# Gate and up matmuls as pairs of 64 rows, with an exchanged copy of the normalised input

## The chip, the cores and the metric

The kernel runs on one core of one Trainium2 chip. The metric is device time in microseconds (us) of one execution, and lower is better. Times given for a kernel are medians over several executions; a profile is one further execution, with its own time.

## The reference, cut to what matters

Two branches work on the same normalised input, and their sum is added to the input. D is 576, S is 2048, F is 4608; all inputs and the output are bf16.

```
x  = A_x                                  # [1, 2048, 576]
xn = layernorm(x)                         # over the last axis
q, k, v = split(xn @ A_wqkv)              # 32 heads of 18
# each position attends to itself and 7 earlier ones, 2 apart
logits[s, w] = q[s] . k[s - 2w] * 18**-0.5      # -1e9 where s - 2w < 0
o = sum_w softmax(logits)[s, w] * v[s - 2w]
g = silu(xn @ B_w_gate)                   # 576 -> 4608
u = xn @ B_w_up                           # 576 -> 4608
out = x + o @ A_wo + (g * u) @ B_w_down   # 4608 -> 576
```

## The kernel before, in words

Tokens are held as 16 rows (`r`) of 128 partitions: token 16p + r is partition p of row r. Four rows make a block `tt` of 512 tokens (`TT`), and there are four blocks.

**First stage.** Each row is normalised, transposed on TensorE (L213) and copied by ScalarE into `xnT`: 128 partitions by 5 groups of features by 2048 tokens. The first four groups hold features 0 to 511. The last 64 features stand twice in the fifth group, on partitions 0 to 63 and on 64 to 127. Then come the K and Q projections (`p_full`, L225, and `p_rem`, L232), row by row, and after them V in four groups of four rows. K and V go to staging buffers that lie in the memory of `hT`; `halo` (L281 to L286) copies them from there, shifted by one partition, into the rings `Kr` and `Vr`, and to a scratch in DRAM (`kv_d`) from which later blocks are read back (`ring_load`, L291). There are three staging buffers in turn, so ScalarE's copy of a V group out of PSUM (L247) waits until the copies out of the buffer that it writes have landed.

**Gate and up.** For each block `tt`, a loop runs over nine chunks `ch` of 512 columns of the 4608. Each chunk has four parts `j` of 128 columns. A part needs gate and up, each [128 columns] x [512 tokens], summed over 576 features: four matmuls of 128 features (`g_full`, L415) and one of 64 (`g_rem`, L425) for each of the two. In `g_rem` gate reads partitions 0 to 63 and up partitions 64 to 127, so that two matmuls stand in the two halves of TensorE's array at the same time. The eight short matmuls of a chunk stand together: parts 0 and 1 do their long matmuls first, then come all the short ones, then the long ones of parts 2 and 3. Gate and up of a part go to the two banks of one PSUM tile (a ring of four tiles of two banks). `g_evac` then applies silu to gate on ScalarE (L431), copies up on ScalarE (L432), and multiplies both on VectorE into `hT` (L433).

**Weights.** `load_gu` brings a chunk's weights into one of two slots of `gu`: 512 rows of gate and of up as [128 partitions, 4, 512] each (L163, L164), and the last 64 rows of gate on partitions 0 to 63 and of up on 64 to 127 (L165, L166). All four are on the queue of SP (SyncE), in program order. The load for chunk it + 2 is issued after the matmuls of chunk `it`, and waits for them. In block 0 two loads of `w_down` (L169) follow behind each.

**VectorE's own work.** The sliding attention is a list of pieces (`Filler`), which `dve.pump` puts between other VectorE work, with costs written out by hand. The list of block tt + 1 is added in chunk 1 of block tt.

**Down and output.** After the nine chunks of a block, the attention's output is transposed (L474, copied by L478), and for each of four rows 36 matmuls of `w_down` (L489) and five of `A_wo` (L492) go into one PSUM tile for each half of the 576 columns. VectorE adds the residual `xr` into a tile `ot` (L498), and SP stores it (L499). `xr` is one buffer, loaded in chunk 4 of each block.

Of the kernel before, what the change touches and what calls it, by code (L numbers as in the profile page):

```python
# [9 lines left out]
bf16 = mybir.dt.bfloat16  # L10
f32 = mybir.dt.float32
ACT = mybir.ActivationFunctionType
ALU = mybir.AluOpType
# [4 lines left out]
P = 128  # L18
H, DH, W, DIL = 32, 18, 8, 2
D = H * DH  # L20
HALF = D // 2
# [8 lines left out]
NTT = R // RT  # L30
TT = RT * P
NRING = HALO + RT
FC = 4
NSLOT = 2
# [31 lines left out]
def kernel(  # L66
# [11 lines left out]
    nc = tc.nc  # L78
# [4 lines left out]
    NCH = NF // FC  # L83

    x_v = A_x.rearrange("b (p r) d -> p (b r) d", r=R)
    out_v = out.rearrange("b (p r) d -> p (b r) d", r=R)

    const = ctx.enter_context(tc.tile_pool(name="const", bufs=1))
    big = ctx.enter_context(tc.tile_pool(name="big", bufs=1))
    tmp = ctx.enter_context(tc.tile_pool(name="tmp", bufs=1))  # L90
# [9 lines left out]
    xnT = big.tile([P, KT, S], bf16, name="xnT")  # L100
# [9 lines left out]
    ssum = big.tile([P, RT, H], f32, name="ssum")  # L110
    gu = big.tile([P, NSLOT, 9, FC * P], bf16, name="gu")
    xr = big.tile([P, RT, D], bf16, name="xr")
    kv_d = dram.tile([2, NTT - 1, P, RT * D], bf16, name="kv_d")


# [17 lines left out]


    nc.gpsimd.memset(eps_t[:], EPS)
    wz = tmp.tile([P, D], bf16, name="ot", tag="ot", bufs=3)
    nc.vector.memset(wz[:], 0.0)

    def load_w3(eng, m):
        src = A_wqkv[:, m * D:(m + 1) * D]  # L140
        eng.dma_start(wq3[m], src[0:512, :].rearrange("(kt kp) n -> kp kt n", kp=P))
        eng.dma_start(wq3r[m][0:64, :], src[512:576, 0:HALF])
        eng.dma_start(wq3r[m][64:128, :], src[512:576, HALF:D])
# [16 lines left out]
    def load_gu(it):  # L160
        ch, slot = it % NCH, it % NSLOT
        fc = slice(ch * FC * P, (ch + 1) * FC * P)
        nc.sync.dma_start(gu[:, slot, 0:4, :], B_w_gate[0:512, fc].rearrange("(kt kp) n -> kp kt n", kp=P))  # L163
        nc.sync.dma_start(gu[:, slot, 4:8, :], B_w_up[0:512, fc].rearrange("(kt kp) n -> kp kt n", kp=P))  # L164
        nc.sync.dma_start(gu[0:64, slot, 8, :], B_w_gate[512:576, fc])  # L165
        nc.sync.dma_start(gu[64:128, slot, 8, :], B_w_up[512:576, fc])  # L166

    def load_wd(ch):
        nc.sync.dma_start(wd[:, ch * FC:(ch + 1) * FC, :],  # L169
                          B_w_down[ch * FC * P:(ch + 1) * FC * P, :].rearrange("(f p) j -> p f j", p=P))  # L170

    def new_ps(name):
        return ps.tile([P, 2, 512], f32, name=name, tag="ps")
# [81 lines left out]
    def p_units(units, hooks):  # L255


        n = len(units) // 2
        ts = []
        for i in range(n):  # L260
            ts.append(new_ps("qkv_ps"))
            p_full(*units[i], ts[i], True)
            hooks[i]()
        for i in range(n, len(units)):
            ts.append(new_ps("qkv_ps"))
        for i, (m, r) in enumerate(units):
            p_rem(m, r, ts[i], i >= n)
        for i in range(n):
            p_evac(*units[i], ts[i])
        for i in range(n, len(units)):  # L270
            p_full(*units[i], ts[i], False)
            p_evac(*units[i], ts[i])
            hooks[i]()
# [20 lines left out]
    dve = Filler()  # L294
# [92 lines left out]
    for r in range(R):  # L387
        p_units([(1, r), (0, r)], [ahead, ahead if r == 2 else none])
        if r == 0:
            nc.sync.dma_start(xc_b[2], x_v[:, 8:12, :])  # L390
            nc.sync.dma_start(xc_b[3], x_v[:, 12:16, :])
            load_w3(nc.sync, 2)
    nc.vector.memset(Kr[0:1, 0:HALO, :], 0.0)
    nc.vector.memset(Vr[0:1, 0:HALO, :], 0.0)
    load_gu(0)
    load_gu(1)
    chain(0)
    for i in range(4):
# [6 lines left out]
    wd_order = [8, 0, 1, 2, 3, 4, 5, 6, 7]  # L405
    ring_ps = {}

    def g_full(tt, ch, j, first):
        slot = (tt * NCH + ch) % NSLOT
        t = ring_ps[j]  # L410
        tok = slice(tt * TT, (tt + 1) * TT)
        fc = slice(j * P, (j + 1) * P)
        for b in range(2):
            for kt in range(4):
                nc.tensor.matmul(t[:, b, :], gu[:, slot, 4 * b + kt, fc], xnT[:, kt, tok],  # L415
                                 start=(first and kt == 0), stop=(not first and kt == 3))

    def g_rem(tt, ch, j, first):
        slot = (tt * NCH + ch) % NSLOT
        t = ring_ps[j]  # L420
        tok = slice(tt * TT, (tt + 1) * TT)
        fc = slice(j * P, (j + 1) * P)
        for b in range(2):
            rows = slice(64 * b, 64 * b + 64)
            nc.tensor.matmul(t[:, b, :], gu[rows, slot, 8, fc], xnT[rows, 4, tok], start=first, stop=not first)  # L425

    def g_evac(ch, j):
        t = ring_ps[j]
        sg = tmp.tile([P, TT], bf16, name="sg", tag="sg", bufs=4)
        uc = tmp.tile([P, TT], bf16, name="uc", tag="uc", bufs=4)  # L430
        nc.scalar.activation(sg[:], t[:, 0, :], ACT.Silu)  # L431
        nc.scalar.copy(uc[:], t[:, 1, :])  # L432
        nc.vector.tensor_tensor(hT[:, ch * FC + j, :], sg[:], uc[:], op=ALU.mult)  # L433

    for tt in range(NTT):
        for ch in range(NCH):
            it = tt * NCH + ch
            for j in (0, 1):
                ring_ps[j] = new_ps("g_ps")
                g_full(tt, ch, j, True)  # L440
            for j in (2, 3):
                ring_ps[j] = new_ps("g_ps")
            g_rem(tt, ch, 0, False)
            g_rem(tt, ch, 1, False)
            g_rem(tt, ch, 2, True)
            g_rem(tt, ch, 3, True)
            g_evac(ch, 0)
            dve.pump(1.4)
            g_evac(ch, 1)
            dve.pump(1.4)  # L450
            g_full(tt, ch, 2, False)
            g_evac(ch, 2)
            dve.pump(1.4)
            g_full(tt, ch, 3, False)
            g_evac(ch, 3)
            dve.pump(1.4)
            if it + NSLOT < NTT * NCH:
                load_gu(it + NSLOT)
            if tt == 0:
                for _ in range(2):  # L460
                    if wd_order:
                        load_wd(wd_order.pop(0))
            if ch == 4:
                nc.sync.dma_start(xr[:], x_v[:, RT * tt:RT * tt + RT, :])
            if ch == 1 and tt < NTT - 1:
                chain(tt + 1)
        dve.drain(lambda: chains[0] > tt)

        def o_transp(pair):
            pt = ps.tile([P, 2, 8 * P], bf16, name="ot_ps", tag="ps")  # L470
            for q in range(2):
                r = RT * tt + 2 * pair + q
                for k, (c0, n) in enumerate(OCH):
                    nc.tensor.transpose(pt[0:n, q, k * P:(k + 1) * P], QO[:, r, c0:c0 + n], ident[:])  # L474
            for q in range(2):
                r = RT * tt + 2 * pair + q
                for a, b, n in ((0, 3, 128), (3, 5, 96)):
                    nc.scalar.copy(oT[0:n, a:b, r * P:(r + 1) * P],  # L478
                                   pt[0:n, q, a * P:b * P].rearrange("p (k t) -> p k t", t=P))

        o_transp(0)
        o_transp(1)
        for sub in range(RT):
            r = RT * tt + sub
            t = new_ps("d_ps")
            for h in range(2):
                cols = slice(h * HALF, (h + 1) * HALF)
                for f in range(NF):
                    nc.tensor.matmul(t[:, h, 0:HALF], hT[:, f, sub * P:(sub + 1) * P], wd[:, f, cols],  # L489
                                     start=(f == 0), stop=False)  # L490
                for k, (c0, n) in enumerate(OCH):
                    nc.tensor.matmul(t[:, h, 0:HALF], oT[0:n, k, r * P:(r + 1) * P], wo[0:n, k, cols],  # L492
                                     start=False, stop=(k == KT - 1))
            dve.pump(8.5)
            ot = tmp.tile([P, D], bf16, name="ot", tag="ot", bufs=3)
            for h in range(2):
                cols = slice(h * HALF, (h + 1) * HALF)
                nc.vector.tensor_tensor(ot[:, cols], t[:, h, 0:HALF], xr[:, sub, cols], op=ALU.add)  # L498
            nc.sync.dma_start(out_v[:, r, :], ot[:])  # L499


# [28 lines left out]
```

## Time and profile before

| | |
|---|---|
| median of 3 executions | 534.65 us (532.63 to 535.03) |
| the profiled execution | 535.35 us, its span 533.2 us |
| TensorE busy | 520.2 us, 98% of the span |
| granted TensorE clock, mean | 0.996 |
| VectorE busy | 333.4 us, 63% |
| ScalarE busy | 222.1 us, 42% |
| DMA | 70.39 MB, mean 132 GB/s |
| gate and up, long matmuls (L415) | x1120, 379 ns each |
| gate and up, short matmuls (L425) | x288, 379 ns each |

The span is the time from the first to the last instruction of the profiled execution; what lies around it is 535.35 - 533.2 = 2.15 us. Matmuls are pipelined: the duration of one (379 ns) is longer than the distance to the next, so that rates are read from distances between starts. A few matmul records are missing (1120 of 1152 long ones are there). "Idle before" is an engine's idle time ahead of an instruction, with what ended it. SPq is SP's sequencer, on which DMAs are issued.

### The profile page before, as it was taken

To read this page: it belongs to the slowest core of one execution; us is meant where nothing else is said; L and a number is where in the kernel's file an instruction comes from. 1 tells how busy PE (TensorE), PEld (TensorE's weight loads), DVE (VectorE), ACT (ScalarE), POOL (GpSimd) and SP (SyncE) were. 2 spreads that over 40 slices of the span, in tenths; PEclk is the share of its full clock that TensorE was granted. 3 is DMA by queue.
4 is the path that set the end of the run, shared out by engine and by line. 5 is a ranking of instruction groups with operands and counts; after the bars stand their busy time and mean duration, and the time that the engine had idled before them with its cause. 6 is when DMAs were issued, how large, how long until landed. Compare 5 with 4: busy or idle time off the path is not lost.

```text
span 533.2 us, 8296 instructions
## 1 busy us (share of the span) xinstructions
PE 520.2 (98%) x3375; PEld 300.8 (56%) x3407; DVE 333.4 (63%) x474; ACT 222.1 (42%) x431; POOL 9.7 (2%) x25
## 2 busy tenths in 40 slices
PE   6999989999999999999999999999999999999997
PEld 2677754444477754444577644444777544445775
DVE  4765977698899868898798127986991121221010
ACT  2677545656440035455600074466400354555000
POOL 6000000000000000000000000000000000000000
PEclk9899999999999999999999999999999999999999
DMA  8332798996620115554601035545200145540000
GB/s 280 119 134 90 217 301 263 339 306 201 216 90 23 57 49 185 177 176 136 222 13 57 23 97 171 171 149 169 90 12 23 58 131 177 184 129 0 12 12 22
DMA packets 58229, 70.39 MB, mean 132 GB/s; under 512 B 3768, under 2 KB 54072, under 8 KB 58192
## 3 DMA queue, kind: packets, MB, share of 16 engines
q1 hardware_dynamic: 56928, 68.55, 40.4%
q0 software_dynamic: 576, 0.66, 0.4%
q10 hardware_dynamic: 688, 0.66, 0.4%
q8 instruction: 26, 0.43, 0.4%
q14 instruction: 11, 0.09, 0.1%
HBM read 58.69 MB, written 5.90 MB: 121 GB/s over the span
## 4 chain that ended last, share of the span: by engine, by line
PE 92%; DMA 5%; SPq 1%; issue 1%; DVE 0%; ACT 0%; DVEq 0%; ACTq 0%
PE g_ps L415 47%; PE d_ps L489 26%; PE g_ps L425 7%; PE qkv_ps L225 6%; PE d_ps L492 4%; DMA gu<-in_B_w_up_dram 2%; DMA Vr<-hT 1%; PE qkv_ps L232 1%; DMA wd<-in_A_x_dram 1%; PE pt L213 1%; PE ot_ps L474 1%; DMA hT<-in_A_wqkv_dram 1%; SPq L282 0%; SPq L286 0%; DVE wd L200 0%
## 5 line engine op out<-in xcount | busy, mean ns | idle before, releaser
L415 PE MATMUL g_ps<-xnT,gu 128*128 128x512 bf16 x1120 | 252.5, 379 | 4.4 <-ACT hT L247 1.8
L415 PEld LDWEIGHTS <-gu 128*128 128x128 bf16 x1152 | 109.8, 98 | 144.0 <-issue 17.3
L431 ACT ACTIVATE sg<-g_ps 128x512 bf16<-128x512 f32 x144 | 87.1, 605 | 157.6 <-PE g_ps L425 123.2
L489 PE MATMUL d_ps<-wd,hT 128*128 128x288 bf16 x1152 | 146.4, 286 | 0.0
L489 PEld LDWEIGHTS <-hT 128*128 128x128 bf16 x1152 | 112.4, 98 | 28.5
L433 DVE TENSOR_TENSOR hT<-sg,uc 128x512 bf16<-128x512 bf16 x144 | 60.4, 420 | 106.8 <-ACT uc L432 106.0
L316 DVE TENSOR_REDUCE PP<-PP 128x64 f32<-128x1152 bf16 x64 | 85.1, 1347 | 0.4
L432 ACT CAST uc<-g_ps 128x512 bf16<-128x512 f32 x144 | 85.1, 591 | 0.0
L498 DVE TENSOR_TENSOR ot<-d_ps,xr 128x288 bf16<-128x288 f32 x32 | 13.1, 451 | 64.6 <-PE d_ps L492 64.6
L225 PE MATMUL qkv_ps<-hT,xnT 128*128 128x288 bf16 x384 | 52.0, 291 | 0.1
L225 PEld LDWEIGHTS <-xnT 128*128 128x128 bf16 x384 | 36.2, 99 | 14.5 <-issue 5.0
L343 DVE TENSOR_TENSOR PP<-Vr,A 128x2304 bf16<-128x2304 bf16 (+1 forms) x35 | 43.4, 1252 | 0.5
L311 DVE TENSOR_TENSOR PP<-QO,Kr 128x2304 bf16<-128x2304 bf16 (+1 forms) x35 | 43.4, 1248 | 0.3
L425 PE MATMUL g_ps<-xnT,gu 64*128 64x512 bf16 x288 | 37.4, 379 | 0.0
L348 DVE TENSOR_TENSOR PP<-PP 128x2304 bf16<-128x2304 bf16 x24 | 32.5, 1355 | 0.4
L431 ACT ACT_TABLE_LOAD x5 | 6.4, 1283 | 54.3 <-PE g_ps L425 54.2
L492 PE MATMUL d_ps<-wo,xnT 128*128 128x288 bf16 (+1 forms) x160 | 24.9, 286 | 0.0
L425 PEld LDWEIGHTS <-gu 64*128 64x128 bf16 x288 | 11.1, 94 | 23.8 <-issue 15.3
L492 PEld LDWEIGHTS <-xnT 128*128 128x128 bf16 (+1 forms) x160 | 15.7, 98 | 3.9
L188 DVE BATCH_NORM_STATS2 stats<-wd 128x6 f32<-128x288 bf16 x32 | 13.0, 449 | 3.8 <-DMA wd<-in_A_x_dram 3.8
L247 ACT CAST hT<-qkv_ps 128x288 bf16<-128x288 f32 x32 | 10.6, 416 | 10.8 <-DMA Vr<-hT 4.9
L336 ACT ACTIVATE PP<-PP 128x1024 f32<-128x1024 f32 x4 | 4.2, 1057 | 24.8 <-DVE PP L332 24.8
(40 smaller groups left out, 167.4 us busy)
## 6 DMA issues: line engine op xcount, KB each, us to landing
gu<-in_B_w_gate_dram SPq DMA_DIRECT2D x36, 512.0 KB, 3.6
gu<-in_B_w_up_dram SPq DMA_DIRECT2D x36, 512.0 KB, 5.1
wd<-in_B_w_down_dram SPq DMA_DIRECT2D x9, 576.0 KB, 5.7
kv_d<-hT SPq DMA_DIRECT2D x6, 576.0 KB, 4.9
gu<-in_B_w_gate_dram SPq DMA_DIRECT2D x36, 64.0 KB, 4.9
gu<-in_B_w_up_dram SPq DMA_DIRECT2D x36, 64.0 KB, 4.5
xr<-in_A_x_dram SPq DMA_DIRECT2D x4, 576.0 KB, 5.4
out_dram<-ot SPq DMA_DIRECT2D x16, 144.0 KB, 1.8
```

Of the source, the lines that this page charges most:

```text
L225: nc.tensor.matmul(t[:, h, 0:HALF], xnT[:, kt, r * P:(r + 1) * P], wq3[m][:, kt, h * HALF:(h + 1) * HALF], start=(first and kt == 0), stop ...
L311: nc.vector.tensor_tensor(prod[:, a:b], QO[:, RT * tt + a:RT * tt + b, :], Kr[:, s:s + b - a, :], op=ALU.mult)
L316: nc.vector.tensor_reduce(L[:, w, rs], prod[:, rs].rearrange("p r (h d) -> p r h d", d=DH), axis=AX.X, op=ALU.add)
L343: nc.vector.tensor_tensor(dst[:, a:b], Vr[:, s:s + b - a, :].rearrange("p r (d h) -> p r d h", h=H), A[:, w, a:b].unsqueeze(2).to_broadcas ...
L348: nc.vector.tensor_tensor(dst, acc, pv, op=ALU.add)
L415: nc.tensor.matmul(t[:, b, :], gu[:, slot, 4 * b + kt, fc], xnT[:, kt, tok], start=(first and kt == 0), stop=(not first and kt == 3))
L425: nc.tensor.matmul(t[:, b, :], gu[rows, slot, 8, fc], xnT[rows, 4, tok], start=first, stop=not first)
L431: nc.scalar.activation(sg[:], t[:, 0, :], ACT.Silu)
L432: nc.scalar.copy(uc[:], t[:, 1, :])
L433: nc.vector.tensor_tensor(hT[:, ch * FC + j, :], sg[:], uc[:], op=ALU.mult)
L489: nc.tensor.matmul(t[:, h, 0:HALF], hT[:, f, sub * P:(sub + 1) * P], wd[:, f, cols], start=(f == 0), stop=False)
L492: nc.tensor.matmul(t[:, h, 0:HALF], oT[0:n, k, r * P:(r + 1) * P], wo[0:n, k, cols], start=False, stop=(k == KT - 1))
```

## The change

All the gate and up matmuls are now short ones of 64 features. The 576 rows of a weight are nine pieces of 64; gate's nine pieces lie on partitions 0 to 63 of a slot and up's nine on partitions 64 to 127. A part `j` is nine pairs: one matmul of gate in the upper half of the array and one of up in the lower half.

A gate piece with an odd number needs features that `xnT` holds on partitions 64 to 127, and an up piece with an even number needs some that it holds on 0 to 63. For these there is `xsw`, a copy of the first four groups of a block of `xnT` with its two halves exchanged, made by two DMAs from SBUF to SBUF: once in the first stage (at r = 5) and then after the gate and up part of each block but the last. The order of the pairs takes those that need no `xsw` first.

`load_gu` becomes two DMAs, one of 64 partitions for gate and one of 64 partitions for up, 576 KB each. The parts of a chunk run one after the other, with `g_evac` and `dve.pump(1.4)` behind each. The buffers `sg` and `uc` go from four to three. The residual is added in place in `xr`, which is then stored, and `ot` is gone; the zeros for the first matmuls lie in `xr` as well.

```diff
+    xsw = big.tile([P, 4, TT], bf16, name="xsw")
...
-    wz = tmp.tile([P, D], bf16, name="ot", tag="ot", bufs=3)
-    nc.vector.memset(wz[:], 0.0)
+    wz = xr[:, 0, :]
+    nc.vector.memset(wz, 0.0)
...
     def load_gu(it):
         ch, slot = it % NCH, it % NSLOT
         fc = slice(ch * FC * P, (ch + 1) * FC * P)
-        nc.sync.dma_start(gu[:, slot, 0:4, :], B_w_gate[0:512, fc].rearrange("(kt kp) n -> kp kt n", kp=P))
-        nc.sync.dma_start(gu[:, slot, 4:8, :], B_w_up[0:512, fc].rearrange("(kt kp) n -> kp kt n", kp=P))
-        nc.sync.dma_start(gu[0:64, slot, 8, :], B_w_gate[512:576, fc])
-        nc.sync.dma_start(gu[64:128, slot, 8, :], B_w_up[512:576, fc])
+        nc.sync.dma_start(gu[0:64, slot], B_w_gate[:, fc].rearrange("(c p) n -> p c n", p=64))
+        nc.sync.dma_start(gu[64:128, slot], B_w_up[:, fc].rearrange("(c p) n -> p c n", p=64))
+
+    def load_xsw(tt):
+        tok = slice(tt * TT, (tt + 1) * TT)
+        nc.sync.dma_start(xsw[0:64], xnT[64:128, 0:4, tok])
+        nc.sync.dma_start(xsw[64:128], xnT[0:64, 0:4, tok])
...
+        if r == 5:
+            load_xsw(0)
...
-    def g_full(tt, ch, j, first):
+    def g_mm(tt, ch, j):
         slot = (tt * NCH + ch) % NSLOT
         t = ring_ps[j]
         tok = slice(tt * TT, (tt + 1) * TT)
         fc = slice(j * P, (j + 1) * P)
-        for b in range(2):
-            for kt in range(4):
-                nc.tensor.matmul(t[:, b, :], gu[:, slot, 4 * b + kt, fc], xnT[:, kt, tok],
-                                 start=(first and kt == 0), stop=(not first and kt == 3))
-
-    def g_rem(tt, ch, j, first):
...
-        for b in range(2):
-            rows = slice(64 * b, 64 * b + 64)
-            nc.tensor.matmul(t[:, b, :], gu[rows, slot, 8, fc], xnT[rows, 4, tok], start=first, stop=not first)
+        lo, hi = slice(0, 64), slice(64, P)
+        order = [(0, 1), (2, 3), (4, 5), (6, 7), (8, 8), (1, 0), (3, 2), (5, 4), (7, 6)]
+        for i, (cg, cu) in enumerate(order):
+            xg = xsw[lo, cg // 2, :] if cg % 2 else xnT[lo, cg // 2, tok]
+            xu = xnT[hi, cu // 2, tok] if cu % 2 or cu == 8 else xsw[hi, cu // 2, :]
+            for b, rows, c, x in ((0, lo, cg, xg), (1, hi, cu, xu)):
+                nc.tensor.matmul(t[:, b, :], gu[rows, slot, c, fc], x, start=(i == 0), stop=(i == 8))
...
-        sg = tmp.tile([P, TT], bf16, name="sg", tag="sg", bufs=4)
-        uc = tmp.tile([P, TT], bf16, name="uc", tag="uc", bufs=4)
+        sg = tmp.tile([P, TT], bf16, name="sg", tag="sg", bufs=3)
+        uc = tmp.tile([P, TT], bf16, name="uc", tag="uc", bufs=3)
...
-            for j in (0, 1):
+            for j in range(FC):
                 ring_ps[j] = new_ps("g_ps")
-                g_full(tt, ch, j, True)
-            for j in (2, 3):
-                ring_ps[j] = new_ps("g_ps")
-            g_rem(tt, ch, 0, False)
-            g_rem(tt, ch, 1, False)
-            g_rem(tt, ch, 2, True)
-            g_rem(tt, ch, 3, True)
-            g_evac(ch, 0)
-            dve.pump(1.4)
-            g_evac(ch, 1)
-            dve.pump(1.4)
-            g_full(tt, ch, 2, False)
-            g_evac(ch, 2)
-            dve.pump(1.4)
-            g_full(tt, ch, 3, False)
-            g_evac(ch, 3)
-            dve.pump(1.4)
+                g_mm(tt, ch, j)
+                g_evac(ch, j)
+                dve.pump(1.4)
...
         dve.drain(lambda: chains[0] > tt)
+        if tt + 1 < NTT:
+            load_xsw(tt + 1)
...
-            ot = tmp.tile([P, D], bf16, name="ot", tag="ot", bufs=3)
             for h in range(2):
                 cols = slice(h * HALF, (h + 1) * HALF)
-                nc.vector.tensor_tensor(ot[:, cols], t[:, h, 0:HALF], xr[:, sub, cols], op=ALU.add)
-            nc.sync.dma_start(out_v[:, r, :], ot[:])
+                nc.vector.tensor_tensor(xr[:, sub, cols], t[:, h, 0:HALF], xr[:, sub, cols], op=ALU.add)
+            nc.sync.dma_start(out_v[:, r, :], xr[:, sub, :])
```

More of the change, by code (lines that the diff above doesn't have):

```diff
@@ L412, in g_full @@
         fc = slice(j * P, (j + 1) * P)
-        for b in range(2):
-            for kt in range(4):
-                nc.tensor.matmul(t[:, b, :], gu[:, slot, 4 * b + kt, fc], xnT[:, kt, tok],
-                                 start=(first and kt == 0), stop=(not first and kt == 3))
-    def g_rem(tt, ch, j, first):
[L419 to L422, printed above, removed]
-        for b in range(2):
-            rows = slice(64 * b, 64 * b + 64)
-            nc.tensor.matmul(t[:, b, :], gu[rows, slot, 8, fc], xnT[rows, 4, tok], start=first, stop=not first)
+        lo, hi = slice(0, 64), slice(64, P)
[5 more added lines that the diff above has]
+                nc.tensor.matmul(t[:, b, :], gu[rows, slot, c, fc], x, start=(i == 0), stop=(i == 8))
     def g_evac(ch, j):
         t = ring_ps[j]
-        sg = tmp.tile([P, TT], bf16, name="sg", tag="sg", bufs=4)
-        uc = tmp.tile([P, TT], bf16, name="uc", tag="uc", bufs=4)
+        sg = tmp.tile([P, TT], bf16, name="sg", tag="sg", bufs=3)
+        uc = tmp.tile([P, TT], bf16, name="uc", tag="uc", bufs=3)
         nc.scalar.activation(sg[:], t[:, 0, :], ACT.Silu)
```

## The prediction, made before the result was known

> **What bounds the kernel now.** I read the page's busy times and its chain of waits first.
>
> ```profile
> span 533.2 us, 8296 instructions
> PE 520.2 (98%) x3375; PEld 300.8 (56%) x3407; DVE 333.4 (63%) x474; ACT 222.1 (42%) x431; POOL 9.7 (2%) x25
> ...
> PE 92%; DMA 5%; SPq 1%; issue 1%; DVE 0%; ACT 0%; DVEq 0%; ACTq 0%
> ```
>
> TensorE (PE) carries 92% of the chain that ends last, so the question is the distance between its matmuls, and whether anything else will be late. For the distances I took the timeline of one chunk in block 1:
>
> ```profile
> 201.20 1.04 PE L425 MATMUL g_ps<-xnT,gu 64*128 64x512 bf16 x8
> ...
> 202.17 7.08 PE L415 MATMUL g_ps<-xnT,gu 128*128 128x512 bf16 x32
> ...
> 204.97 0.37 SPq L163 DMA_DIRECT2D gu<-in_B_w_gate_dram  x1
> ...
> 205.83 0.37 SPq L164 DMA_DIRECT2D gu<-in_B_w_up_dram  x1
> ...
> 206.81 0.59 SPq L166 DMA_DIRECT2D gu<-in_B_w_up_dram  x1
> ...
> 209.19 1.04 PE L425 MATMUL g_ps<-xnT,gu 64*128 64x512 bf16 x8
> ```
>
> Columns are start, length, engine, line. A chunk lasts 209.19 - 201.20 = 7.99 us. Long matmuls follow each other at (7.08 - 0.38) / 31 = 0.216 us (0.38 is the length of one, 379 ns). Eight short ones are four pairs: (1.04 - 0.38) / 3 = 0.22 us from pair to pair. A pair costs what one long matmul costs, so nine pairs are no more work than eight long ones and a pair. What is lost now are the changes between the two kinds: short to long 0.97 - 4 x 0.216 = 0.106 us, long to short 7.02 - 32 x 0.216 = 0.108 us, together 0.21 us per chunk.
>
> **What goes on TensorE.** 36 chunks x 0.21 = 7.6 us are removed; two changes per block stay, into pairs and back to whole-array transposes: 4 x 0.21 = 0.8 us. A chunk becomes 36 x 0.216 = 7.78 us. Sum: -6.8 us, all on the path.
>
> Can the sequencer keep up? A pair is four instructions (two weight loads), 54 ns each. In the K and Q stage one row takes 2.70 us (runs of L225 start at 28.69, 31.38, 34.08 in the chain) for 25 matmuls and 25 weight loads, 54 ns each, with no gap on PE. It holds there, and I book nothing; the trace shows no row beyond that rate in a long run.
>
> **What comes instead: the refill of a slot.** Now gate's large load leaves at 204.97, when the last gate matmul is through, 0.86 us before up's. Interleaved pairs free both at the end, so both leave at about 205.83, 0.2 us after the chunk's end (202.17 + 16 x 0.216 = 205.63). They must land before the next chunk is over, 7.78 us after that end. Today the last small load leaves at 206.81 and lands 4.5 us later (page's median for L166): 211.3, 5.7 us after the end, with 2.3 us to spare. But the new loads fill 64 partitions each, and the trace has no long transfer of that shape. The nearest rows, in windows of the DMA columns (share, GB/s, at the end of each line):
>
> ```profile
> 312.00:313.00 1.00, 1.00 (x7) 0.41 (x6) 0.42 (x1) 0.18 (x1) 0.00 (x0) 1.00 1.03 363
> 313.00:314.00 1.00, 0.95 (x5) 0.47 (x5) 0.00 (x0) 0.00 (x0) 0.00 (x0) 1.00 1.07 366
> ...
> 36.25:37.50 1.25, 1.25 (x15) 0.76 (x12) 1.13 (x4) 1.04 (x2) 0.00 (x0) 1.00 1.07 269
> 38.50:39.50 1.00, 1.00 (x13) 0.61 (x12) 0.59 (x3) 0.57 (x3) 0.00 (x0) 1.00 1.05 429
> 72.00:74.00 2.00, 2.00 (x21) 1.44 (x21) 1.93 (x3) 0.00 (x0) 0.00 (x0) 1.00 1.02 229
> ```
>
> All are saturated (share about 1). The first two are today's weight loads over 128 partitions. The third is the K halo copy over 112 partitions, shifted by one; the fourth the store of the same buffer over 128. Same packets of 4608 B, but their mean length is 291 ns against 180: where the partitions do not spread evenly, packets wait for each other and the rate falls to 269/429 = 0.63. The fifth, V halos, falls to 229/429 = 0.53. Bounds for the new loads: 366 GB/s (no loss; today's 64-row remainders, 64 packets each at the end of a refill, have a median packet of about 51 ns there against 46 before, nearly that) down to 0.53 x 366 = 195. I take 0.63, 230 GB/s: a long load that uses one half of the partitions is nearer to the uneven copy than to a few packets among others.
>
> [...]
>
> A chunk's weights are 1.18 MB: 3.2 us at 366, 5.1 at 230, 6.0 at 195. Start and landing around the data are today 211.3 - 205.83 - 3.2 = 2.3 us. So the refill lands 0.2 + 2.3 + 5.1 = 7.6 us after the chunk's end, against 7.78: just in time. L164's landings scatter (median 5.1 us, some over 6), so I book 0.13 us of waiting per refill: 21 refills in blocks 1 to 3, 2.7 us; at 366 nothing, at 195 0.2 + 2.3 + 6.0 - 7.78 = 0.7 us, 0.8 with the scatter.
>
> **Block 0** also loads `w_down`, 1.18 MB per chunk over 128 partitions, behind each refill on the same queue: 5.1 + 3.2 = 8.3 us of transfers per 7.78 us of chunk. For four chunks 0.55 us each, 1.6 us for the read-back of K (0.59 MB) among them, 0.4 us for the rest: +4.2 us.
>
> **The start of gate and up.** The first two chunks' weights (2.36 MB) are queued at 58 us, ahead of V's halo copies, and the DMA share is about 1 from 57 to 83 us. ScalarE waits for one of those copies, and TensorE for ScalarE:
>
> ```profile
> 75.75 2.52 ACT L247 CAST hT<-qkv_ps 128x288 bf16<-128x288 f32 x8 [4.91 <-DMA Vr<-hT]
> ...
> 76.50 3.61 PE L415 MATMUL g_ps<-xnT,gu 128*128 128x512 bf16 x15 [1.83 <-ACT hT L247]
> ```
>
> At 230 GB/s the weights take 10.3 us instead of 6.4, and the copies behind them land 3.8 us later. Two issues per chunk instead of four let SP reach the copies earlier; that can give between nothing and the stall's 1.83 us, and I take 0.8. Sum +3.0 us; without the rate loss -0.8. One more cost can hide here: after PE's idle time at 10 to 12 us the granted clock was 0.50 at 14 to 16 us. If a stall of 5 us did that, some 3.4 us at half clock would cost up to 1.7 us; a stall of 1.83 us does not today (clock 1.00 after it), so it stays in the range alone.
>
> **What I cost at nothing.** `xsw(0)`, two copies of 256 KB, falls into SP's free time between 26.4 and 35.0 us and is needed at 76. Later ones wait for the block's last pair; behind them on SP stand the output stores and read-backs, due 5 us later or more, and the 41 us of the down projection cover them (uncovered: about 4 us each, three times). `g_evac`: 1.1 us of ScalarE per part of 1.94. With three buffers the multiply may be 3.9 us late; the worst piece ahead of it (L331) is 1.9. The exponential with two table loads, 1.28 + 1.06 + 1.28 = 3.6 us, fits in the 4.6 us until the PSUM tile is wanted (uncovered: up to 1 us, four times). VectorE has 0.42 us plus a piece of 1.35 us per part, under 1.94. The residual in place has the same shape, and `xr` is reloaded over 30 us after its last store, which lands in 1.8 us.
>
> **Sum.** -6.8 + 2.7 + 4.2 + 3.0 = +3.1 us. The profiled execution would go from 535.35 to 538.5 (span 536.3); it stands 0.7 us above the median, so the median goes from 534.65 to 537.8.
>
> **Rivals.** (1) The halves load at the old rate: no late refill, start -0.8, so -6.8 - 0.8: 527.0. For it: the remainders lose little, and gate and up travel at the same time, one half each. Against: the halo rows. Chance 0.34; this is the one that ends faster, and it decides from about 250 GB/s upwards, where a chunk's weights take 4.7 us, nothing is late in blocks 1 to 3, block 0 costs 1.5 us and the start 9.4 - 6.4 - 0.8 = 2.2: -3.1 us. (2) The loads fall to 195 GB/s: 0.8 us on 21 refills (17), block 0 with 9.2 us of transfers per chunk (4 x 1.4 + 1.6 + 2.4 = 9.6), start 12.1 - 6.4 - 0.8 = 4.9: -6.8 + 31.5, 559; at 215 by the same steps (7.3, 6.3, 3.8) 545. Chance 0.13. (3) Pairs do not run at 0.216 us in a long stream, because the sequencer or the two halves get in each other's way, so that the change does not do what it says: at 0.24 us, 1296 pairs x 24 ns = 31 us, 559 with no late load. Only four pairs in a row are seen now; the 54 ns row speaks against it. Chance 0.08. The forecast has the remaining 0.45.
>
> **How the numbers follow.** 0.5% of 534.65 is 2.7 us, about what a measurement of this kernel can tell from no change. The forecast's own range is 532 to 546, and its sum lies at the edge of the band: of its 0.45 I give 0.29 to slower, 0.13 to the same, 0.03 to faster. With rival 1 faster (0.33, and 0.01 the same) and rivals 2 and 3 slower (0.21): faster 0.36, same 0.14, slower 0.50. The range, 526.5 to 552, holds rival 1 and the forecast and leaves out the upper part of rivals 2 and 3.
>
> **What would show it.** In the profile after: gate and up as 2592 matmuls in pairs 0.216 us apart and a chunk of 7.78 us where nothing is late (right for the TensorE term); windows of a refill at about 230 GB/s with share 1, and landings near 7.4 us after issue; PE waiting for `gu`'s DMA, most in block 0; the wait at 75 us grown to some 5 us. Wrong, towards rival 1, if refills run at 360 GB/s and land in under 6 us; towards rival 3 if pairs are further apart with the weights long landed.

## The result and the profile after

The changed kernel takes 560.57 us (median of four executions, 560.10 to 565.00) beside 534.78 us for the kernel before on the same chip: a ratio of 1.0494, 95% interval 1.0459 to 1.0530. The forecast was 537.8 us with a range up to 552. Its direction was right; its size was not, by 23 us.

The profiled execution is the slowest of the four: 565.0 us, span 563.2; the other spans are 558.3 to 559.0. About 4 us of what it shows belong to that execution alone. The page of the changed kernel, first the span and the busy times, then the granted clock in 40 slices, then the chain of waits:

```profile
span 563.2 us, 10562 instructions
...
PE 526.7 (94%) x4559; PEld 306.6 (54%) x4559; DVE 336.7 (60%) x474; ACT 225.6 (40%) x431; POOL 9.7 (2%) x25
...
PEclk9899989999899999999999999999999999999999
...
PE 71%; DMA 26%; SPq 1%; DVE 0%; issue 0%; ACT 0%; DVEq 0%
```

The chain that ends last was 92% TensorE and 5% DMA. Now 26% of it are DMAs, and two slices of the first third show a clock below 0.9 beside the one at the very start. The view of waits names the DMA (total us, times, longest):

```profile
PEld L427 <- DMA gu<-in_B_w_up_dram: 33.1, 24, 4.2
...
PE g_ps L427 <- DMA gu<-in_B_w_up_dram: 22.0, 19, 3.9
```

It is up's, the second of the two new loads, in every wait for these weights but one of 0.3 us. Here is a refill in block 2, in the timeline:

```profile
343.38 0.59 SPq L165 DMA_DIRECT2D gu<-in_B_w_gate_dram  x1
343.96 7.45 PEld L427 LDWEIGHTS <-gu 64*128 64x128 bf16 x72 [0.90 <-DMA gu<-in_B_w_up_dram]
343.97 1.25 PE L427 MATMUL g_ps<-xnT,gu 64*128 64x512 bf16 x9 [0.41 <-DMA gu<-in_B_w_up_dram]
344.06 0.60 SPq L166 DMA_DIRECT2D gu<-in_B_w_up_dram  x1
...
351.73 0.59 SPq L165 DMA_DIRECT2D gu<-in_B_w_gate_dram  x1
351.86 2.06 PEld L427 LDWEIGHTS <-gu 64*128 64x128 bf16 x22 [0.44 <-DMA gu<-in_B_w_up_dram]
```

A chunk ends at 343.19. Gate's load leaves 0.19 us later and up's 0.68 us behind it; the trace has up's data landed at 351.81, and TensorE goes on at 351.86. From the chunk's end that is 8.6 us, where a chunk of TensorE lasts 7.78. The transfer in windows (DMA share and GB/s are the last two columns):

```profile
346.00:347.00 1.00, 1.00 (x13) 0.41 (x10) 0.00 (x0) 0.88 (x2) 0.00 (x0) 1.00 1.11 258
347.00:348.00 1.00, 1.00 (x12) 0.49 (x10) 0.78 (x2) 0.19 (x1) 0.00 (x0) 1.00 1.10 190
348.00:349.00 1.00, 1.00 (x14) 0.45 (x10) 0.96 (x2) 0.94 (x2) 0.00 (x0) 1.00 1.13 223
349.00:350.00 1.00, 1.00 (x12) 0.43 (x10) 1.00 (x1) 0.13 (x1) 0.00 (x0) 1.00 1.13 197
```

The engines are saturated and move a mean of (258 + 190 + 223 + 197) / 4 = 217 GB/s, against 363 to 366 before. Over all refills the page has, with the median us from issue to landing at the end of a line:

```profile
gu<-in_B_w_gate_dram SPq DMA_DIRECT2D x36, 576.0 KB, 5.8
gu<-in_B_w_up_dram SPq DMA_DIRECT2D x36, 576.0 KB, 8.2
```

Where the 30.0 us between the two spans went, by the starts of matmuls in the two traces: V's last projection ends 1.3 us later, and the first gate matmul comes 4.9 us behind it instead of 2.1 (start: +4.1). Block 0 lasts 90.5 us from its first to its last gate or up matmul, blocks 1 to 3 last 73.5, 73.4 and 75.2, where all four had 71.85 (+18.6 and +6.5). From the start of a block's last matmul to the start of the next block's first it is 41.74 us instead of 41.54 (+0.7 with what follows the last block).

### The profile page after: what moved, and what is told of

It reads as the page before. It is cut to its first block, busy times and chain, and to the rows that moved or that the text cites. A ratio compares the mean times of both kernels' runs of the same rounds, so it can differ in the third digit from the quotient of the medians.

```text
span 563.2 us, 10562 instructions
## 1 busy us (share of the span) xinstructions
PE 526.7 (94%) x4559; PEld 306.6 (54%) x4559; DVE 336.7 (60%) x474; ACT 225.6 (40%) x431; POOL 9.7 (2%) x25
## 4 chain that ended last, share of the span: by engine, by line
PE 71%; DMA 26%; SPq 1%; DVE 0%; issue 0%; ACT 0%; DVEq 0%
PE g_ps L427 32%; PE d_ps L479 25%; DMA gu<-in_B_w_up_dram 22%; PE qkv_ps L230 7%; PE d_ps L482 3%; DMA Vr<-hT 2%; PE qkv_ps L237 1%; SPq L165 1%; DMA wd<-in_A_x_dram 1%; PE ot_ps L464 1%; PE pt L218 1%; DMA hT<-in_A_wqkv_dram 1%; DVE wd L205 0%; DVE stats L193 0%; ACT QO L246 0%
## 5 line engine op out<-in xcount | busy, mean ns | idle before, releaser
L427 PE MATMUL g_ps<-xnT,gu 64*128 64x512 bf16 x1440 | 210.4, 383 | 26.6 <-DMA gu<-in_B_w_up_dram 22.0
L427 PEld LDWEIGHTS <-gu 64*128 64x128 bf16 x2592 | 126.9, 95 | 190.0 <-DMA gu<-in_B_w_up_dram 33.1
L427 PE MATMUL g_ps<-xsw,gu 64*128 64x512 bf16 x1152 | 174.1, 381 | 0.0
L434 ACT CAST uc<-g_ps 128x512 bf16<-128x512 f32 x144 | 83.7, 581 | 0.0
L487 DVE TENSOR_TENSOR xr<-d_ps,xr 128x288 bf16<-128x288 f32 x32 | 13.1, 451 | 65.8 <-PE d_ps L482 65.8
L252 ACT CAST hT<-qkv_ps 128x288 bf16<-128x288 f32 x32 | 10.6, 415 | 13.6 <-DMA Vr<-hT 7.7
L224 ACT COPY xnT<-pt 128x640 bf16<-128x640 bf16 x15 | 10.4, 691 | 7.9 <-PE pt L218 7.9
```

The source lines that it names most:

```text
L427: nc.tensor.matmul(t[:, b, :], gu[rows, slot, c, fc], x, start=(i == 0), stop=(i == 8))
L487: nc.vector.tensor_tensor(xr[:, sub, cols], t[:, h, 0:HALF], xr[:, sub, cols], op=ALU.add)
```

## Experiments

Each ratio is against the kernel before, run beside it (medians of 534.10 to 535.37 us). Runs 5 to 8 were on another chip than the other runs.

**1. The old loads under the new matmuls.** `load_gu` as before the change, all else as changed.

```
-    nc.sync.dma_start(gu[0:64, slot], B_w_gate[:, fc].rearrange("(c p) n -> p c n", p=64))
-    nc.sync.dma_start(gu[64:128, slot], B_w_up[:, fc].rearrange("(c p) n -> p c n", p=64))
+    nc.sync.dma_start(gu[:, slot, 0:4, :], B_w_gate[0:512, fc].rearrange("(kt kp) n -> kp kt n", kp=P))
+    nc.sync.dma_start(gu[:, slot, 4:8, :], B_w_up[0:512, fc].rearrange("(kt kp) n -> kp kt n", kp=P))
+    nc.sync.dma_start(gu[0:64, slot, 8, :], B_w_gate[512:576, fc])
+    nc.sync.dma_start(gu[64:128, slot, 8, :], B_w_up[512:576, fc])
```

> The changed kernel with the four old weight loads (128 partitions for 512 rows) and nothing else turned back; the pairs, the exchanged copy and all the rest stay. The pieces then lie elsewhere in a slot, so the sums are those of other features: this leaves the right sums out, the instructions are the same. Theory (the 64-partition loads alone cost the time): no late refill, pairs 0.216 us apart, chunk 7.78 us, blocks of 70.2 us, 525 to 530 us. Rival (the pairs, their order, or the gate load's lost head start cost the time): refills or pairs still late, 545 us or more.

Measured: 529.32 us, ratio 0.9890 (0.9856 to 0.9925), span 524.9. The chain and the landings, from its page:

```profile
PE 93%; DMA 5%; SPq 1%; DVE 0%; ACT 0%; issue 0%; DVEq 0%; ACTq 0%
...
gu<-in_B_w_gate_dram SPq DMA_DIRECT2D x36, 512.0 KB, 3.7
gu<-in_B_w_up_dram SPq DMA_DIRECT2D x36, 512.0 KB, 5.1
```

In the changed kernel the loads land after 5.8 and 8.2 us. Every block now lasts 69.94 us, 1.91 less than before the change. With the 0.20 us more at each change of blocks this is -7.6 + 0.7 = -6.9 us: the TensorE term of the prediction, which had -6.8. It also settles what was costed at nothing: the exchanged copy, the residual in place, three buffers and the new order of `g_evac` are all in this kernel and cost nothing that shows.

**2. The new loads alone,** in the kernel before; the matmuls stay as they were.

```
-    nc.sync.dma_start(gu[:, slot, 0:4, :], B_w_gate[0:512, fc].rearrange("(kt kp) n -> kp kt n", kp=P))
-    nc.sync.dma_start(gu[:, slot, 4:8, :], B_w_up[0:512, fc].rearrange("(kt kp) n -> kp kt n", kp=P))
-    nc.sync.dma_start(gu[0:64, slot, 8, :], B_w_gate[512:576, fc])
-    nc.sync.dma_start(gu[64:128, slot, 8, :], B_w_up[512:576, fc])
+    nc.sync.dma_start(gu[0:64, slot], B_w_gate[:, fc].rearrange("(c p) n -> p c n", p=64))
+    nc.sync.dma_start(gu[64:128, slot], B_w_up[:, fc].rearrange("(c p) n -> p c n", p=64))
```

> The kernel before with the two new 64-partition loads and nothing else; its matmuls read the slot as before, so they find other rows there: the right sums are left out, the instructions of all engines but SP are the same. Theory: the loads bring the waits into the kernel before too. A chunk of 7.98 us leaves 0.2 us more than one of 7.78, so 1.4 us less waiting in each later block; the long waits of block 0, the start and the lowered clock stay: 554 to 566 us. Rival (loads are not the cause): 533 to 538 us.

Measured: 560.64 us, ratio 1.0464 (1.0433 to 1.0494). This is the time of the whole change (560.57). So the loads alone bring the loss, and with them in place the 7 us that pairs save on TensorE do not show in the time: in the profiles block 0 lasts 85.5 us here and 90.5 in the changed kernel, blocks 1 to 3 last 74.3 to 76.2 here and 73.4 to 75.2 there.

**3. Fewer `w_down` loads per chunk in block 0.**

```
-for _ in range(2):
+for _ in range(2 if ch == 0 else 1):
```

> The changed kernel with the loads of w_down spread over block 0: two in its first chunk and one in each later one, instead of two in each of the first four. Theory (in block 0 transfers are the bound: 1.18 MB at about 205 GB/s and 1.18 MB at 366 need 9 us per chunk of 7.78): with 0.59 MB the same steps need 7.4 us, so most of block 0's 13.8 us of waiting and its two later spells of half clock go: 545 to 551 us. Rival (block 0 waits for its refills by their own rate alone, as the later blocks do): within 3 us of the changed kernel.

Measured: 554.35 us, ratio 1.0350 (1.0305 to 1.0396). Block 0 falls from 90.5 to 83.9 us; blocks 1 to 3 stay at 72.7 to 73.3. So some 6 us of block 0's loss are refills that stand behind `w_down`; waits of 2.7 and 2.6 us remain, and the time lies between the theory's and the rival's.

**4. Up's load on ScalarE's queue,** so that both halves of the array can be filled at once.

```
-    nc.sync.dma_start(gu[64:128, slot], B_w_up[:, fc].rearrange("(c p) n -> p c n", p=64))
+    nc.scalar.dma_start(gu[64:128, slot], B_w_up[:, fc].rearrange("(c p) n -> p c n", p=64))
```

> The changed kernel with up's load issued from ScalarE's queue and gate's from SP's, so that both halves of a slot have a queue of their own. Theory A (an engine works through one queue's transfers in order, so that all 16 engines fill the same half at a time; two queues let them alternate): refills at 300 GB/s or more, landing within 6 us, 526 to 533 us. Theory B (two halves at once stay as slow as one after the other): within 5 us of the changed kernel. [...]

Measured: 561.71 us, ratio 1.0491 (1.0432 to 1.0549): no gain. The issues stand 0.1 us apart (341.47 and 341.57 in block 2), so both loads are under way together; windows of that refill:

```profile
344.00:345.00 1.00, 1.00 (x14) 0.44 (x10) 0.00 (x0) 0.94 (x2) 0.00 (x0) 1.00 1.11 242
345.00:346.00 1.00, 1.00 (x12) 0.43 (x10) 0.83 (x2) 0.14 (x1) 0.00 (x0) 1.00 1.12 191
346.00:347.00 1.00, 1.00 (x12) 0.49 (x10) 0.96 (x2) 0.99 (x2) 0.00 (x0) 1.00 1.11 229
347.00:348.00 1.00, 1.00 (x14) 0.42 (x10) 1.00 (x1) 0.13 (x2) 0.00 (x0) 1.00 1.12 195
```

214 GB/s in the mean, as with one queue, and gate still lands after 5.6 us and up after 8.1: they land one after the other. That an engine works through one queue's transfers in order was the author's assumption; no run shows it. The argument for rival 1, that gate and up travel at the same time, one half each, falls here.

**5. The second chunk's weights issued later,** behind V's projections.

```
 load_gu(0)
-load_gu(1)
 chain(0)
 for i in range(4):
     p_units(...)
+load_gu(1)
```

> The second chunk's gate and up weights (1.18 MB) are issued behind V's projections instead of ahead of them; all else as in the changed kernel. Theory: at the start it is only the amount queued ahead of V's halo copies that counts, and the half clock at 79.6 to 86.4 us comes from the 4.7 us wait in front of it. Then the first gate matmul starts within 1 us of the last V matmul (76.5 to 77 instead of 80.6), no half clock follows it, and some 4 + 3 us are gained, of which the second chunk, now later, gives back up to 2: 554 to 557 us. Rival: the loss belongs to the bytes on the queue, whatever their order, and comes back as a wait in front of the second chunk: 559 to 562 us, with a first stall of 4 us or more inside block 0.

Measured: 555.14 us, ratio 1.0384 (1.0335 to 1.0434), 5.4 us below the changed kernel. The first gate matmul starts 0.2 us after V's last one instead of 4.9, with no half clock behind it. So the start's loss was the amount queued ahead of V's halo copies. TensorE then stands idle for 2.8 and 2.3 us in front of the second chunk's two loads, at 83 to 89 us, and a half-clock window of 6.8 us follows that instead: the theory's time was right, but the half clock moved rather than went.

**6. Odd and even partitions instead of halves.** The same two loads, the same number of partitions and of packets.

```
-    nc.sync.dma_start(gu[0:64, slot], B_w_gate[:, fc].rearrange("(c p) n -> p c n", p=64))
-    nc.sync.dma_start(gu[64:128, slot], B_w_up[:, fc].rearrange("(c p) n -> p c n", p=64))
+    gv = gu[:, slot].rearrange("(p q) c n -> q p c n", q=2)
+    nc.sync.dma_start(gv[0], B_w_gate[:, fc].rearrange("(c p) n -> p c n", p=64))
+    nc.sync.dma_start(gv[1], B_w_up[:, fc].rearrange("(c p) n -> p c n", p=64))
```

> Each load still fills 64 partitions with the same packets from the same rows of the weights, but gate's go to the even partitions of the whole array's 128 and up's to the odd ones, instead of the lower and the upper half. The matmuls are those of the changed kernel, so their sums mix gate and up rows; the time is that of all its work. Theory A: it is the half that makes the load slow. Then a refill runs at about 350 GB/s, no PE wait for gu beyond 1 us in blocks 1 to 3, and the time is that of the changed kernel with the old loads, 527 to 532 us. Rival B: a load over 64 partitions is slow wherever they lie: about 210 GB/s and 558 to 563 us.

Measured: 527.29 us, ratio 0.9863 (0.9824 to 0.9902): theory A. Two windows of a refill and the landings:

```profile
332.00:333.00 1.00, 1.00 (x13) 0.41 (x10) 1.00 (x3) 0.34 (x1) 0.00 (x0) 1.00 1.09 375
333.00:334.00 1.00, 1.00 (x12) 0.49 (x10) 1.00 (x1) 0.80 (x2) 0.00 (x0) 1.00 1.05 359
```

```profile
gu<-in_B_w_gate_dram SPq DMA_DIRECT2D x36, 576.0 KB, 4.4
gu<-in_B_w_up_dram SPq DMA_DIRECT2D x36, 576.0 KB, 5.6
```

A load over 64 partitions runs at 359 to 375 GB/s if they are spread over the whole array, and at 217 if they are one half of it. Nothing else differs between the loads, so the half is the cause. It is the cause in block 0 too: with the same queue and the same bytes block 0 lasts 70.9 us here, and blocks 1 to 3 last 69.94. Why a half is slower no run shows.

**7. Crosswise pairs.** Gate and up change halves between two groups of pairs, so that `load_gu` is the one before the change and `xsw` falls away. The memset waits for the first group of a part, and the second group for the memset, since in the second group each half of the array adds to the PSUM bank that the other half wrote in the first. No run leaves this order out. The code is shortened, and its comments stand here only; rows 0 to 63 are what the expectation calls the lower half.

```
-for i, (cg, cu) in enumerate(order):
...
+if first:      # (bank, piece) on rows 0-63, (bank, piece) on rows 64-127, group of xnT
+    todo = [(0, kt, 1, 4 + kt, kt) for kt in range(4)] + [(0, 8, 1, 8, 4)]
+else:
+    todo = [(1, 4 + kt, 0, kt, kt) for kt in range(4)]
...
+for j0 in (0, 2):
+    for j in (j0, j0 + 1):
+        ring_ps[j] = new_ps("g_ps")
+        g_pairs(tt, ch, j, True)     # ends with nc.gpsimd.memset(relay[0:1, 2*j:2*j+2], 0.0)
+    for j in (j0, j0 + 1):
+        g_pairs(tt, ch, j, False)
+        g_evac(ch, j)
+        dve.pump(1.4)
```

> A version meant to keep the pairs and the old loads, with the reference's sums: first five pairs with gate in the lower half and up in the upper, then four with up in the lower and gate in the upper, so that no exchanged copy is needed; an order between the two is kept by a tiny memset on GpSimd, behind which five pairs of the next tile lie. Theory: 1296 pairs at 0.216 us as in the changed kernel, refills as before the change, and no copies: 526 to 530 us (the changed kernel with the old loads gave 529.3). Rival: the relay over GpSimd takes longer than the 1.1 us of five pairs; at 0.3 us late, 72 times, that is 22 us and about 550 us, with waits of PE on POOL in the chain.

Measured: 528.98 us, ratio 0.9897 (0.9865 to 0.9929), blocks of 70.32 and three of 69.94 us. The wait over GpSimd costs nothing.

**8. The kernel before with the second chunk later** (the edit of run 5).

> The kernel before, with the second chunk's loads issued behind V's projections. Theory: the 1.83 us that PE waits for V's halo copies at 75 us go away and the second chunk still lands in time (it is due 7.8 us after the first starts, and at 366 GB/s takes 3.2 us and 2.3 us around the data): 532.5 to 533.5 us. Rival: the second chunk, issued behind V's halo copies and ahead of w_down, is late, and the gain is given back: 534.5 to 536 us.

Measured: 535.93 us, ratio 1.0020 (0.9994 to 1.0046): the rival. The first gate matmul follows V's last by 0.1 us instead of 2.1, but waits of 1.7 and 0.7 us for the second chunk come back, which end at 84.3 and 86.0 us, and block 0 lasts 74.5 us instead of 71.85.

**9. Matmuls in the wait.**

```
 ring_ps[j] = new_ps("g_ps")
+if tt == 0 and ch >= 2 and j == 0:
+    for i in range(8):
+        for b, rows in ((0, slice(0, 64)), (1, slice(64, P))):
+            nc.tensor.matmul(ring_ps[j][:, b, :], ident[rows, :], xnT[rows, 0, 0:TT], start=True, stop=True)
 g_mm(tt, ch, j)
```

> The changed kernel, with eight pairs of 64 rows that compute nothing of use (their sums are overwritten) ahead of chunks 3 to 9 of block 0, 1.73 us each, so that PE works through part of the wait for the refill. Theory: the clock halves after PE has been idle for some 3 us, and the two half-clock windows inside block 0 (110 and 145 us) cost 3.4 us on the path; with shorter waits they stay away, and block 0 goes from 90.5 to 87 us, 557 us in all, less what the added pairs cost where the wait is shorter than they are. Rival: in block 0 the queue of transfers is never empty, so its end is set by the bytes; work saved by the full clock turns into waiting, and the time stays at 560 to 562 us with the clock at 1.0.

Measured: 558.90 us, ratio 1.0459 (1.0424 to 1.0495), an interval that overlaps the changed kernel's. Block 0 lasts 88.8 us; one half-clock window is left inside it (121 us) besides the one at its start. One window and 1.7 us less fits the theory, which expected both to go, but it doesn't exclude the rival. What the half clock inside block 0 costs by itself stays open. The "some 3 us" of the theory was the author's estimate: in the changed kernel's profile the half clocks at 110.3 and 144.5 us stand beside waits of 2.60 and 3.93 us.

**10 and 11. Crosswise pairs, the second chunk's loads after V's second or third group.**

```
 for i in range(4):
     p_units(...)
+    if i == 1:        # run 10; i == 2 in run 11
+        load_gu(1)
```

> Crosswise pairs with the old loads, and the second chunk's loads issued after the second of the four groups of V's projections instead of ahead of the first. Theory: half of V's halo copies go ahead of the second chunk, the copy that ScalarE waits for is among them, and the second chunk, due 7.8 us after the first starts, still lands in time: the 1.96 us wait at the start goes and nothing comes back, 526.5 to 528 us, 1 to 2 us below the crosswise version as it was. Rival: the copy that is waited for belongs to the third group, behind the second chunk, and the wait only moves: 528.5 to 530 us.

> The same with the second chunk's loads issued after the third group of V's projections. Theory: the wait at the start goes, but the second chunk comes later: between nothing and the 2.7 us of stalls that it cost when issued behind all four groups: 526.5 to 529 us. Rival: as late as behind all four: 529 to 531 us.

Measured: 527.54 us (0.9849, 0.9821 to 0.9878) and 526.63 us (0.9845, 0.9816 to 0.9874), the theory in both. In both the first gate matmul follows V's last by 0.2 us, and block 0 lasts 69.94 and 70.24 us. The page of run 11, and a stretch of its timeline:

```profile
PE 97%; DMA 2%; DVE 0%; ACT 0%; DVEq 0%; issue 0%
```

```profile
189.73 8.58 PE L427 MATMUL g_ps<-xnT,gu 64*128 64x512 bf16 x78
...
191.32 0.09 POOL L434 MEMSET relay<- 1x2 f32 x1 [2.72 <-PE g_ps L427]
```

TensorE has 97% of the chain and never stops for the memset, which lasts 0.09 us. These two are 7.8 and 8.7 us below the kernel before in the medians; between them the difference is too small to tell.

## Why the prediction was wrong, point by point

The terms of the sum beside what the two profiled executions show (the start and the blocks as above, and 69.94 us taken from run 1 as a block without late loads):

| term | booked | measured |
|---|---|---|
| TensorE | -6.8 | -7.6 + 0.7 = -6.9 |
| refills, blocks 1 to 3 | +2.7 | 3.6 + 3.5 + 5.2 = +12.2 |
| block 0 | +4.2 | 90.46 - 69.94 = +20.5 |
| start | +3.0 | 2.8 + 1.3 = +4.1 |
| sum | +3.1 | +29.9 |

The medians lie 25.8 us apart; the other 4 us belong to the profiled executions. Most of them are in the refills: in runs 3, 5 and 9, whose blocks 1 to 3 are the same program, these blocks cost +8.8, +8.1 and +9.7 us instead of +12.2.

**TensorE: right,** shown by run 1; pairs follow each other at 0.216 us over all 1296 of them where no load is late. Rival 3 is out.

**The rate: nearly right.** 230 GB/s was taken from the halo rows, 217 came. The halo row itself was near in part by luck: it is a copy over 112 partitions of both halves, and run 6 shows that a load to partitions of both halves need lose nothing (359 to 375 GB/s), so its rate has another cause, which no run tests. Its packets are longer, 291 ns against 180; that packets wait for each other where partitions do not spread evenly was the author's reading of this, and is not shown.

**The step that failed first is the fixed part of a refill:** "Start and landing around the data are today 211.3 - 205.83 - 3.2 = 2.3 us". 205.83 is the issue of up's load; gate's had left at 204.97, so part of the 3.2 us of data was already on its way. Counted from gate's issue the fixed part is 211.3 - 204.97 - 3.2 = 3.1 us; in the changed kernel's refill shown above it is 351.81 - 343.38 - 5.4 = 3.0 us. And the new loads do not both leave at the chunk's end: up's stands 0.68 us behind gate's, inside that part. With 3.1 and 217 GB/s (5.4 us) the step gives 0.2 + 3.1 + 5.4 = 8.7 us, where 8.6 was measured and 7.6 predicted. So refills were not "just in time" but 0.8 us late, and TensorE waits that long about once in two chunks: a chunk that waits frees its slot later, and the refill behind it then has the wait as well as the chunk to land in. 21 refills cost 0.58 us each instead of 0.13 (0.39 to 0.46 in runs 3, 5 and 9). Even at the forecast's own 230 GB/s the mended step gives 8.4 us, 0.6 late. The forecast stood 0.2 us from the edge, 7.6 against 7.78, where an error of 1 us decides whether TensorE waits at all.

**The largest miss is block 0, mis-sized by 16 us.** The waits between chunks and the half clock, in the timeline of the changed kernel:

```profile
110.66 2.31 PE L427 MATMUL g_ps<-xnT,gu 64*128 64x512 bf16 x9 [2.60 <-DMA gu<-in_B_w_up_dram]
...
131.86 1.25 PE L427 MATMUL g_ps<-xnT,gu 64*128 64x512 bf16 x9 [2.38 <-DMA gu<-in_B_w_up_dram]
...
143.90 1.80 PE L427 MATMUL g_ps<-xnT,gu 64*128 64x512 bf16 x9 [3.93 <-DMA gu<-in_B_w_up_dram]
```

and the transfers in windows of 8 us:

```profile
100.00:108.00 8.00, 7.88 (x72) 3.42 (x72) 7.30 (x15) 3.55 (x7) 0.00 (x0) 1.00 1.11 254
108.00:116.00 8.00, 5.41 (x38) 2.10 (x38) 0.43 (x1) 5.04 (x6) 0.00 (x0) 0.79 1.08 294
...
132.00:140.00 8.00, 7.97 (x72) 3.40 (x68) 4.70 (x7) 3.38 (x7) 0.00 (x0) 1.00 1.11 218
```

From 92 to 148 us the DMA engines are saturated at a mean of 240 GB/s. In that time go six refills (7.1 MB), all of `w_down` (5.3), the read-back of K and `xr` (0.6 each): 13.6 MB, 56.5 us, while six chunks of TensorE last 46.7. The prediction did not name `xr`, and took 366 GB/s for all that is not a refill; with 32.6 us for the refills at 217 GB/s, the other 6.5 MB had some 24 us, about 270 GB/s (an estimate: the split is not measured). That is 10 us late instead of the 4.2 booked. The rest is the order: a refill that stands behind `w_down` lands up to 13.9 us after its issue. The waits between the chunks of block 0 sum to 14.0 us. Run 3 shows the queue's part, and run 6 that both hang on the halves: there the windows from 92 to 108 us move 328 to 330 GB/s, and block 0 is 1.0 us late in all.

The half clock was booked at nothing and put into the range with 1.7 us. By the trace it stands at 79.6 to 86.4, 110.3 to 113.7 and 144.5 to 147.9 us, at a granted 0.50; in it TensorE worked 5.8 + 3.1 + 3.4 us, and half of that, 6.1 us, is its cost if nothing else hides it (14.0 + 6.1 = 20.1 of the 20.5). That a stall of 5 us might do this was seen in the prediction and not taken.

**The start: right.** The wait for V's halo copies grew by 2.8 us where 3.0 was booked:

```profile
79.89 2.52 ACT L252 CAST hT<-qkv_ps 128x288 bf16<-128x288 f32 x8 [7.71 <-DMA Vr<-hT]
...
80.64 2.32 PE L427 MATMUL g_ps<-xnT,gu 64*128 64x512 bf16 x10 [4.63 <-DMA Vr<-hT]
```

Run 6 bears out the 0.8 us taken for fewer issues: with two loads per chunk at the full rate the first gate matmul comes 1.4 us behind V's last one, 0.7 less than before the change. The 1.3 us on top are a longer half-clock window early in the execution (below), which no edit made.

**Rivals.** Rival 2 had 559 us, near the result, but at 195 GB/s, which did not come; at 215 it had 545. Rival 1 had 527.0 for two loads per chunk at the old rate: that is what run 6 gives (527.29), and near what the pairs give under the old loads (529.32, and 526.63 crosswise with the start mended).

## What to carry to other kernels

Before a layout puts a matrix on one half of the partitions to suit TensorE's row tiles, the refill that fills it has to be costed by its own rate, here 217 GB/s against 363 to 366; the halves can change places in the matmuls instead, and the loads stay whole (526.63 to 528.98 us in runs 7, 10 and 11). A refill's time is counted from its first issue to its last landing, and where it comes within 1 us of the time it has, the forecast should be taken from the late side. What stands on the same queue in the worst stage, all of it, decides there, not the mean over the kernel.

## What the runs showed that was not expected

A load's rate goes by which 64 partitions it fills (359 to 375 GB/s for every second one, 217 for one half), and a second queue does not help (214).

The granted clock falls to 0.50 for 3.4 or 6.8 us behind some waits of TensorE and not behind others, and the length of the wait alone does not tell which: 2.60 us were enough at 110.66 us, and 2.73 us at 106.79 us in run 3 were not. In the changed kernel's profile the half-clock windows after the first 20 us start at 79.61, 110.33 and 144.47 us, 9 and 10 times 3.413 us apart. What goes with them is TensorE's idle time inside one stretch of such a grid. Three stretches, with TensorE's busy time behind the length, the first two of the changed kernel and the third of run 3:

```profile
106.92:110.33 3.41, 1.15 (x12) 0.29 (x7) 1.02 (x3) 2.52 (x4) 0.00 (x0) 1.00 1.09 258
...
127.40:130.81 3.41, 2.08 (x20) 0.75 (x16) 2.91 (x4) 2.15 (x4) 0.00 (x0) 1.00 1.11 229
```

```profile
102.65:106.06 3.41, 1.41 (x14) 0.53 (x10) 1.28 (x3) 2.52 (x5) 0.00 (x0) 1.00 1.10 241
```

The first has 2.3 us idle, and a half clock follows it; the others have 1.3 and 2.0 us, since the waits there lie across two stretches, and none follows. In the changed kernel's profile, from 20 to 515 us and outside the half-clock windows, a half clock follows the three stretches with 2.26, 2.85 and 3.41 us idle and none of those with 1.78 us or less.

The same thing makes executions differ: in the first 20 us the half clock lasts 3.4 us before the change, 6.8 us in the changed kernel's profile and is absent in runs 1 and 6, and the last matmul of V's projections starts at 74.4, 75.7, 72.5 and 72.7 us. That is up to 3 us between executions, 0.6% of the time. No edit is needed for it: of 14 executions of the kernel before beside runs 5 to 8, three with a mean clock of 0.993 took 535.70 to 537.49 us, and three with 0.999 or more 532.49 to 533.19 us.
